# Threshold attention into an RWKV feed-forward: probabilities of 15 of 32 jobs turned on VectorE and by DMA instead of on TensorE

## Chip, core and metric

The kernel runs on one core of one Trainium2 chip. The metric is the device time of one execution in microseconds. Below, PE is TensorE's matmul, PEld its weight load, DVE VectorE, ACT ScalarE, POOL GpSimd and SP the queue of SyncE, which issues every DMA of this kernel. L667 is line 667 of the kernel before; the changed kernel has its own line numbers, and its lines are named as such.

## What is computed

Attention over 8 batches, 8 heads, 576 tokens and 64 columns a head, in which each score below its row's maximum less tau is dropped, and then an RWKV feed-forward over the 512 columns of all heads:

```python
scores = q @ k.T / sqrt(64)
thresh = max(scores, axis=-1) - tau
attn = softmax(where(scores >= thresh, scores, -1e9))
x = (attn @ v), heads side by side            # 8 x 576 x 512
x_prev = x shifted by one token
xk = mu_k * x + (1 - mu_k) * x_prev
xr = mu_r * x + (1 - mu_r) * x_prev
k = maximum(xk @ w_k, 0)                      # 512 -> 1024
out = sigmoid(xr @ w_r) * (k * k @ w_v)
```

All inputs are float32. Products whose rounding matters are made from a high and a low part (fp32r) in three matmuls, or, for attn @ v, in float32 matmuls, each of which the hardware runs as two instructions.

## The kernel before

**Jobs and units.** A job is one pair of heads of one batch; batches 0 and 1 are cut into two jobs a pair, which makes 40 jobs, and 32 pairs in all (the title counts pairs). A job's units are P units, 128 queries of both heads (a score tile of 128 x 576 for each head), and, once a pair, a T unit, the last 64 queries of both heads stacked to 128 rows. Two P units (256 queries) make a group; the T unit goes with one of the two groups.

**A unit's way.** operands() loads q and k of the pair (tile raw), scales, splits into hi and lo (L466, L476) and stacks them by eight DMAs a job into st1 and st2 (L495). scores() multiplies them into the PSUM tile s (L559; for the T unit L534, six matmuls of 288 columns with bd as weights). softmax() takes the row maximum on DVE (L593), the threshold and the exponential on ACT (L601, L609), drops and sums on DVE (L617), inverts the sum (L628, L629) and scales the probabilities p on POOL (L643). turn_pair() then turns p, since attn @ v needs the keys on the partitions: per P unit nine PE transpositions of 128 x 128 (L667), four a head for keys 64 to 575 (the main part) and one for the first 64 keys of both heads (the tail), into PSUM; two copies of 128 x 512, one on ACT (L685) and one on DVE (L687), bring the main part into the tile pm, and one ACT copy the tail into pl. turn_last() does it for the T unit. attend() multiplies pm and pl with v (L747): per group 10 float32 matmuls, 20 instructions, of 256 columns, or 320 where the T unit's 64 queries are in the same tile; DVE copies the result into xT (L687).

**Feed-forward.** ffn_chunk() works on 256 tokens of a batch: POOL differences (L840), DVE mixes into the tile mk (L849), ACT and POOL split into xk and xr (L862, L870), then PE with w_k (L892, 256 columns), w_r (L934) and w_v (L956, 512 columns), and one DMA for 128 rows of output (L972). There are 18 chunks.

**Order.** No engine's order is written by hand. Each step is added with an assumed duration and a key; Plan.order() is a list scheduler that repeatedly takes the step that can start first by these assumptions, ties and near ties (SOFT) by key, and places buffers. The instructions are then issued in that order, and each engine runs its own in order. PE steps of the attention have keys lowered by 1000, so they go ahead of feed-forward steps that could start at the same time. Steps with until (L1012, the fillers) are transpositions of the identity, placed on PE only where the plan sees a gap in the first 100 us.

Of the kernel before, what the change touches and what calls it, by code (L numbers as in the profile page):

```python
# [17 lines left out]
W_MAX = 2.0 ** (0x8F - 127) * (1 + 0x6FFFFF / 2.0**23)  # L18

# [29 lines left out]
class Plan:  # L49
# [4 lines left out]
    SOFT = {"DVE": 0.3, "ACT": 0.3}  # L54
    IDLE = 0.5
# [58 lines left out]
    def order(self, loose=()):  # L114
# [48 lines left out]
        while sum_ < total:  # L163
# [60 lines left out]
def tile_threshold_attention_then_rwkv_ffn(  # L224
# [33 lines left out]
    NE = NTB + 1  # L258
    assert ST == D and NPAIR == NCT and B % NTB == 0
# [10 lines left out]
    W0, W1, W2, W3, AVK = 3.0, 3.5, 50.0, 2.0, 4.5  # L270
    PREP, PB, VB, COLD, EARLY = 8, 2, 2, -1, 30
    EV = ("ACT", 0.49), ("DVE", 0.6)
    KMAX, KEXP, KMASK = 0.0, 0.0, 0.5
# [156 lines left out]
    def operands(job, key):  # L430
        b, hp, nq = job["b"], job["hp"], job["nq"]
        W = nq + 2 * ST + SM
        raw = job["raw"] = sbuf("raw", [P, WM], F32, 2)
# [49 lines left out]
        job["st"] = [(sbuf("st1", [P, WM], FR, 3), sbuf("st2", [P, S], FR, 3)) for _ in range(2)]  # L483
        for h in range(2):
# [4 lines left out]
            for dst, rows, src, n, r in (  # L489
                (t1, up, hi, W, (hi, None)),  # L490
                (t2, dn, hi, nq, (hi, None)),
                (t1, dn, lo, W, (lo, None)),
                (t2, up, lo, nq, (lo, 0)),
            ):
                fn = (lambda dst=dst, rows=rows, src=src, n=n, sl=sl: SY.dma_start(  # L495
                    dst.get()[rows, 0:n].bitcast(F32), src.get()[sl, 0:n].bitcast(F32)
                ))
                add("DMA", DQ, fn, reads=[r], writes=[(dst, rows.start)], key=key - PREP, kb=n // 4)
# [4 lines left out]
    def scores(unit, ss, key):  # L503
        job, c = unit["job"], unit["c"]
        raw, nq = job["raw"], job["nq"]
# [3 lines left out]
        def keys(y, z):  # L509
            k0 = nq + (ST if unit["kind"] == "P" and y == 0 else 0)  # L510
            return slice(k0 + z * HS, k0 + (z + 1) * HS)

        if unit["kind"] == "T" and not job["plain"]:

            hi, lo = job["hi"], job["lo"]
            for v_, src in enumerate((raw, lo)):
                for h in range(2):
# [4 lines left out]
                        lambda v_=v_, src=src, sl=sl: A.activation(  # L522
                            bd.get()[sl, v_, sl], src.get()[sl, nq - ST : nq].bitcast(F32), AF.Copy
# [6 lines left out]
            for j, (v_, r) in enumerate(prods):  # L530

                def mm(j=j, v_=v_, r=r):
                    for z in range(2):
                        PE.matmul(ss[1].get()[:, z, 0:HS], bd.get()[:, v_], r.get()[:, keys(1, z)], start=(j == 0), stop=(j == 2))  # L534

                add("PE", 0.264, mm, reads=[bd, r], writes=[ss[1]], key=key - 1000, lat=0.44)
            return
        if unit["kind"] == "T" or job["plain"]:

            last = unit["kind"] == "T"  # L540

            def both():
                for z in range(2):
                    for h in range(2):
                        hr = slice(h * D, (h + 1) * D)
                        o = ss[1].get()[hr, z, 0:HS] if last else ss[h].get()[:, z, 0:HS]
                        q = slice(nq - ST, nq) if last else slice(c * P, (c + 1) * P)
                        PE.matmul(o, raw.get()[hr, q], raw.get()[hr, keys(h, z)], start=True, stop=True)
# [20 lines left out]
    def softmax(unit):  # L569
# [4 lines left out]
        p = unit["p"] = sbuf("p", [P, 2, S], F32, PB)  # L574
        ss = {y: psum("s", [P, 2, 512], 2) for y in ys}
        scores(unit, ss, float(n))
        for y in ys:
# [3 lines left out]
            def sv(s=s):  # L581
                return s.get()[:, :, 0:HS]

            def pv(y=y):
                return p.get()[:, y].rearrange("p (a b) -> p a b", a=2)

            def col(j, y=y):
# [5 lines left out]
                lambda sv=sv, col=col: V.tensor_reduce(col(0), sv(), axis=AX.XY, op=ALU.max, negate=True),  # L593
# [17 lines left out]
                writes=[(p, y)],  # L611
# [9 lines left out]
                writes=[(p, y), (sm, (2, y))],  # L621
# [17 lines left out]
        for y in ys:  # L639
# [4 lines left out]
                    p.get()[:, y], p.get()[:, y], sm.get()[:, 3, y : y + 1], 0.0, op0=ALU.mult, op1=ALU.add  # L644
                ),
                reads=[(sm, (3, y))],
                writes=[(p, y)],
                key=n - 1.0,
# [4 lines left out]
    def group(job, g):  # L653
        if g not in job["groups"]:
            job["groups"][g] = (
                sbuf("pm", [P, 2, 4, CH + ST], F32, 2),
                sbuf("pl", [P, CH + ST], F32, 2),
# [3 lines left out]
    def transposes(p, y, at, key, to):  # L661
# [3 lines left out]
        def mm():  # L665
            for c, o in enumerate(at):
                PE.transpose(  # L667
                    pt.get()[:, c, :], p.get().rearrange("p y s -> p (y s)")[:, o : o + P], ident.get()
                )

        occ = 0.109 * len(at) * (2.3 if key < COLD else 1)
# [4 lines left out]
            reads=[*((p, z) for z in y), ident],  # L676
# [12 lines left out]

    def turn_pair(unit):  # L690
        n, job, p, c = (unit[j] for j in ("n", "job", "p", "c"))
        pm, pl = group(job, c // 2)
        cs = slice(c % 2 * P, (c % 2 + 1) * P)
        for y in range(2):
            pt = transposes(p, (y,), [y * (S + ST) + j * P for j in range(4)], n + y - 1.0, [(pm, (y, c % 2))])
            evict(
                *EV[y if n > EARLY else 0],
                pt,
                lambda y=y: pm.get()[:, y, :, cs],
                lambda pt=pt: pt.get(),  # L700
                [(pm, (y, c % 2))],
                n + y - 2.0,
            )
        pt = transposes(p, (0, 1), [SM], n + 0.1, [(pl, c % 2)])
        evict("ACT", 0.2, pt, lambda: pl.get()[:, cs], lambda: pt.get()[:, 0], [(pl, c % 2)], n - 1.0)

    def turn_last(unit):
        n, job, p = unit["n"], unit["job"], unit["p"]
        pm, pl = group(job, job["tg"])
        cs = slice(CH, CH + ST)  # L710
# [386 lines left out]
```

## Time and profile before

| | |
|---|---|
| median of 3 runs | 1066.53 us (1066.46 to 1067.39) |
| the profiled execution | 1066.21 us, its span 1064.4 us, mean granted clock 0.995 |
| busy, share of span | PE 97%, PEld 81%, DVE 70%, ACT 69%, POOL 55% |
| idle time on PE | 33.9 us (1064.4 less 1030.5) |
| PE transpositions of p (L667) | 1312 |
| DMA | 118.48 MB, SP's queue 42.9% of 16 engines' span |

Busy time counts an instruction from its start to a modelled end. Matmuls overlap, so the mean of one is longer than what it takes of PE in a row; for that the chain of waits is read, which merges instructions that follow each other without a gap.

### The profile page before, as it was taken

To read this page: it belongs to the slowest core of one execution; us is meant where nothing else is said; L and a number is where in the kernel's file an instruction comes from. 1 tells how busy PE (TensorE), PEld (TensorE's weight loads), DVE (VectorE), ACT (ScalarE), POOL (GpSimd) and SP (SyncE) were. 2 spreads that over 40 slices of the span, in tenths; PEclk is the share of its full clock that TensorE was granted. 3 is DMA by queue.
4 is the path that set the end of the run, shared out by engine and by line. 5 is a ranking of instruction groups with operands and counts; after the bars stand their busy time and mean duration, and the time that the engine had idled before them with its cause. 6 is when DMAs were issued, how large, how long until landed. Compare 5 with 4: busy or idle time off the path is not lost.

```text
span 1064.4 us, 19978 instructions
## 1 busy us (share of the span) xinstructions
PE 1030.5 (97%) x7021; PEld 859.1 (81%) x7021; DVE 744.0 (70%) x1816; ACT 731.8 (69%) x1557; POOL 582.2 (55%) x610
## 2 busy tenths in 40 slices
PE   8999989999999899999999999999999999999998
PEld 6677677787877788878879788787889788888887
DVE  6998777777877878779778888757878497222220
ACT  5889766788777687876777768757786567444442
POOL 4789656555554565555565546464556354344441
PEclk9999999999999999999999999999999999999999
DMA  6895574655444444445545346433643050000000
GB/s 219 238 322 140 135 187 123 167 131 148 126 106 126 106 109 115 119 101 130 126 104 124 98 113 140 100 85 81 163 107 89 13 124 15 20 20 22 20 20 20
DMA packets 44354, 118.48 MB, mean 111 GB/s; under 512 B 7392, under 2 KB 10976, under 8 KB 44256
## 3 DMA queue, kind: packets, MB, share of 16 engines
q1 hardware_dynamic: 44256, 117.21, 42.9%
q8 instruction: 57, 0.93, 0.4%
q14 instruction: 41, 0.34, 0.1%
HBM read 46.14 MB, written 9.44 MB: 52 GB/s over the span
## 4 chain that ended last, share of the span: by engine, by line
PE 80%; DVE 7%; ACT 6%; DMA 3%; issue 2%; POOL 1%; SPq 0%; POOLq 0%; ACTq 0%; DVEq 0%
PE w L892 18%; PE w L956 14%; PE w L747 13%; PE s L559 12%; PE w L667 11%; PE w L934 8%; PE s L534 2%; DVE p L617 2%; ACT p L609 2%; DVE mk L849 2%; DVE sm L593 2%; DMA st<-lo 2%; PE w L1012 1%; ACT pm L685 1%; ACT L609 1%
## 5 line engine op out<-in xcount | busy, mean ns | idle before, releaser
L643 POOL TENSOR_SCALAR p<-p,sm 128x576 f32<-128x576 f32 x288 | 218.8, 771 | 204.5 <-DVE sm L629 130.5
L617 DVE SCALAR_TENSOR_TENSOR p<-s,sm,p 128x576 f32<-128x576 f32 x288 | 233.0, 814 | 64.3 <-ACT p L609 61.9
L892 PE MATMUL w<-xk,wk 128*128 128x256 f32 x1728 | 238.8, 286 | 1.7 <-ACT r L900 1.1
L593 DVE TENSOR_REDUCE sm<-s 128x1 f32<-128x576 f32 x288 | 210.3, 751 | 36.9 <-PE s L559 27.3
L956 PE MATMUL w<-wv,k 128*128 128x512 f32 x864 | 219.8, 396 | 1.7 <-ACT pm L685 1.7
L892 PEld LDWEIGHTS w<-xk,wk 128*128 128x128 f32 x1728 | 219.0, 190 | 2.9 <-ACT r L900 1.3
L609 ACT ACTIVATE p<-s,sm 128x576 f32<-128x576 f32 x288 | 210.6, 732 | 0.5
L667 PE MATMUL w<-ident,p 128*128 128x128 f32 x1312 | 193.2, 276 | 7.5 <-POOL p L643 3.5
L667 PEld LDWEIGHTS w<-ident,p 128*128 128x128 f32 x1312 | 151.6, 141 | 43.0 <-POOL p L643 16.9
L956 PEld LDWEIGHTS w<-wv,k 128*128 128x128 f32 x864 | 155.9, 188 | 29.7 <-ACT pm L685 2.3
L685 ACT ACTIVATE pm<-w 128x512 f32<-128x512 f32 x174 | 102.9, 593 | 76.6 <-PE w L667 75.2
L870 POOL TENSOR_TENSOR xk<-mk,xk 128x512 fp32r<-128x512 f32 x72 | 92.7, 1288 | 111.2 <-ACT xk L862 104.8
L747 PE MATMUL w<-pm,v 128*64 128x256 f32 (+1 forms) x1024 | 142.2, 416 | 1.7 <-DVE pm L687 1.1
L849 DVE SCALAR_TENSOR_TENSOR mk<-m,mu_sb,xT 128x256 f32<-128x256 f32 x128 | 87.5, 723 | 80.0 <-POOL xk L870 78.8
L915 POOL TENSOR_TENSOR k<-r,k 128x512 fp32r<-128x512 f32 x72 | 93.2, 1294 | 89.2 <-ACT k L905 82.2
L601 ACT ACTIVATE sm<-sm,small 128x1 f32<-128x1 f32 x288 | 83.5, 290 | 74.6 <-DVE sm L593 73.3
L559 PE MATMUL s<-st 128*128 128x288 f32 x496 | 115.2, 314 | 13.5 <-issue 5.1
L476 POOL TENSOR_TENSOR lo<-raw,hi 128x576 fp32r<-128x576 f32 (+2 forms) x76 | 105.6, 1408 | 33.2 <-ACT hi L466 25.3
L747 PEld LDWEIGHTS w<-pm,v 128*64 128x64 f32 x1024 | 68.5, 138 | 57.5 <-issue 8.8
L934 PE MATMUL w<-wr,xk 128*128 128x512 f32 x432 | 110.1, 396 | 0.2 <-ACT pm L685 0.2
L559 PE MATMUL s<-st,st 128*128 128x288 f32 x496 | 109.0, 301 | 0.0
L559 PEld LDWEIGHTS s<-st 128*128 128x128 f32 x496 | 79.0, 190 | 31.3 <-issue 14.8
(66 smaller groups left out, 1142.3 us busy)
## 6 DMA issues: line engine op xcount, KB each, us to landing
raw<-in_qk SPq DMA_DIRECT2D x24, 608.0 KB, 4.8
st<-hi SPq DMA_DIRECT2D x48, 304.0 KB, 3.2
st<-lo SPq DMA_DIRECT2D x48, 304.0 KB, 4.2
v<-in_v SPq DMA_DIRECT2D x40, 320.0 KB, 4.0
out<-sg SPq DMA_DIRECT2D x32, 256.0 KB, 2.1
st<-hi SPq DMA_DIRECT2D x48, 144.0 KB, 3.4
st<-lo SPq DMA_DIRECT2D x48, 144.0 KB, 3.7
wk<-in_w_k SPq DMA_DIRECT2D x8, 512.0 KB, 6.4
```

The source lines that it names most:

```text
L559: PE.matmul(ss[y].get()[:, z, 0:HS], l.get()[:, c * P : (c + 1) * P], r.get()[:, keys(y, z)], start=(j == 0), stop=(j == 1),)
L593: lambda sv=sv, col=col: V.tensor_reduce(col(0), sv(), axis=AX.XY, op=ALU.max, negate=True),
L609: lambda sv=sv, pv=pv, col=col: A.activation(pv(), sv(), AF.Exp, bias=col(0)),
L617: lambda sv=sv, pv=pv, col=col: V.scalar_tensor_tensor(pv(), sv(), col(1), pv(), op0=ALU.is_ge, op1=ALU.mult, accum_out=col(2)),
L643: lambda y=y: G.tensor_scalar(p.get()[:, y], p.get()[:, y], sm.get()[:, 3, y : y + 1], 0.0, op0=ALU.mult, op1=ALU.add),
L667: PE.transpose(pt.get()[:, c, :], p.get().rearrange("p y s -> p (y s)")[:, o : o + P], ident.get())
L685: fn = lambda: A.activation(out_(), in_(), AF.Copy)
L747: PE.matmul(o.get()[hs, 0:n], vt.get()[:, c, hs], pt[:, 0:n], start=(c == 0), stop=(c == 4))
L849: V.scalar_tensor_tensor(d.get()[:, y, o : o + n], diff.get()[:, y, o : o + n], mu_sb.get()[:, j, hc + y : hc + y + 1], prv[:, hc + y], op ...
L892: PE.matmul(h.get()[:, f], l, r, start=(ct == 0 and i == 0), stop=(ct == NCT - 1 and i == 2))
L934: PE.matmul(z.get(), l, r, start=(ct == 0 and i == 0), stop=(ct == NCT - 1 and i == 2))
L956: PE.matmul(vps.get(), l, r, start=(ft == 0 and i == 0), stop=(ft == NFT - 1 and i == 2))
```

## The change

**Moved jobs.** For batches 3 to 7 and the first three of the four pairs (15 pairs) the main part is no longer turned by PE. DVE turns both heads' 512 main columns of a unit in place, each 32 x 32 block by itself (one STREAM_TRANSPOSE of 128 x 2 x 512 a unit, 60 in all), and when both units of a group are done, 16 DMAs a group from SP carry the rows of blocks to their partitions in pm, each 32 partitions of four pieces of 512 bytes, 64 KB (480 in all). The host orders queries and the rows of v to match. The tail is still turned by PE. For the other 17 pairs PE still turns everything, into the new layout.

**Layout.** p holds a whole group now (two buffers, each for two units, where it was one unit each), pm is 128 x 8 x 2 x 128, and the T unit has its own tiles pml and pll; attend() therefore has 10 matmuls of 256 columns and, with a T unit, 10 more of 64 columns, where it had 10 of 320. The T unit's scores are three matmuls of 512 and three of 64 columns, where they were six of 288. Where a job has a T unit, its 64 queries come first, and st1 and st2 lose those 64 columns.

**Buffers and numbers.** raw has one buffer, not two (job 1 borrows k2); the tile mk is gone: the second mix is written over the difference m, the first into a buffer of r; r keeps two. Constants of the planner differ (SOFT, IDLE, W1 2.5 instead of 3.5, KMAX 1 instead of 0, the attend key's 2.5 instead of 1.5); the planner is told 0.5 us for the issue of one of the 16 DMAs. The T unit leads in the second half jobs.

Counts by the two orders: PE transpositions of p 1312 to 832; PE fillers of three 63 to 52; copies of 128 x 512 into pm on DVE 114 to 54 and on ACT 142 to 82; T-unit copies 32 on ACT as before; DMAs on SP gain the 480; activation table loads 26 to 30.

The core of the diff:

```diff
+def moved(b, hp):
+    return b >= 3 and hp < 3
...
-    SOFT = {"DVE": 0.3, "ACT": 0.3}
-    IDLE = 0.5
+    SOFT = {"DVE": 0.15, "ACT": 0.4, "POOL": 0}
+    IDLE = 0.7
...
-                s.end = max(t + 3.5, pipe + 2.5)
+                s.end = max(t + s.occ + 3.0, pipe + 2.5)
...
+    KTURN, KMOVE, RB, DMOVE = 1, 4, 2, 0.5
+    KMAX, KEXP, KMASK = 1, 0, 0.5
...
-                    for z in range(2):
-                        PE.matmul(ss[1].get()[:, z, 0:HS], bd.get()[:, v_], r.get()[:, keys(1, z)], start=(j == 0), stop=(j == 2))
+                    k = r.get()[:, nq : nq + S]
+                    main = k[:, ST:]
+                    if job["moved"]:
+                        main = main.rearrange("p (r c a) -> p c r a", c=4, a=Q)
+                    for o, x in ((ss[1].get()[:, 0], main), (ss[1].get()[:, 1, 0:ST], k[:, 0:ST])):
+                        PE.matmul(o, bd.get()[:, v_], x, start=(j == 0), stop=(j == 2))
...
+        if job["moved"]:
+
+            def turn():
+                x = strided(p.get()[:, t * PW :], 2, SM)
+                V.transpose(x, x)
+
+            add("DVE", 1.13, turn, writes=[(p, (t, y, "m")) for y in range(2)], key=n - KTURN)
...
+        if job["moved"] and t == 1:
+            for r in range(NQ):
+
+                def move(r=r):
+                    for i in range(NQ):
+                        SY.dma_start(
+                            pm.get()[r * Q : (r + 1) * Q, 2 * i : 2 * i + 2].rearrange("p t h n -> p (t h) n"),
+                            strided(p.get()[i * Q : (i + 1) * Q, r * P :], 4, P),
+                        )
+
+                add("DMA", NQ * DMOVE, move, reads=[(p, (z, y, "m")) for z in range(2) for y in range(2)], writes=[(pm, (r, "moved"))], key=n - KMOVE, kb=256)
...
-            for c in cs:
-                for h in range(2):
-                    hs = slice(h * D, (h + 1) * D)
-                    pt = pl.get() if c == 4 else pm.get()[:, h, c]
-                    PE.matmul(o.get()[hs, 0:n], vt.get()[:, c, hs], pt[:, 0:n], start=(c == 0), stop=(c == 4))
+            for a, e, pm, pl in parts:
+                for c in cs:
+                    for h in range(2):
+                        hs = slice(h * D, (h + 1) * D)
+                        pt = pl.get() if c == 4 else pm.get()[:, :, h, c * Q : (c + 1) * Q]
+                        PE.matmul(o.get()[hs, a:e], vt.get()[:, c, hs], pt, start=(c == 0), stop=(c == 4))
...
-            for j in range(2):
-                d = sbuf("mk", [P, 2, CH], F32, 1)
+            for j in (1, 0):
+                d = sbuf("r", [P, 2, CH], F32, RB) if j else diff
```

**PE before, a job of batch 3.** From the attend of one group (pm_0_4966 with the T unit's columns) over the next T unit's scores (s_0_5198) to the nine transpositions of a P unit's probabilities (p_1_5174); wv are weights of the feed-forward.

```order
L747 MATMUL w_1_5176<-pm_0_4966,v_1_4650 64x320 x8
L747 MATMUL w_1_5176<-pl_0_4973,v_1_4650 64x320 x2
L667 MATMUL w_0_5196<-ident_66,p_0_5078 128x128
L534 MATMUL s_0_5198<-hi_0_4869,bd_81 128x288 x2
L534 MATMUL s_0_5198<-lo_0_4888,bd_81 128x288 x2
L534 MATMUL s_0_5198<-hi_0_4869,bd_81 128x288 x2
L559 MATMUL s_1_5211<-st1_1_4890 128x288 x2
L559 MATMUL s_1_5211<-st1_1_4890,st2_1_4901 128x288 x2
L667 MATMUL w_2_5221<-ident_66,p_1_5174 128x128 x4
L956 MATMUL w_3_5112<-wv50_0_1665,k2_0_4731 128x512 x3
L667 MATMUL w_0_5238<-ident_66,p_1_5174 128x128 x4
L667 MATMUL w_1_5250<-ident_66,p_1_5174 128x128
```

The main part's transpositions are the two rows with x4, between other work.

**PE now, the first moved job (batch 3).** The next T unit's scores (s_0_4685), the scores ahead of them, and behind them all that PE still turns of a P unit of this job (p_1_4593), the tail.

```order
L574 MATMUL s_1_4674<-st1_1_4309,st2_1_4318 128x288 x2
L547 MATMUL s_0_4685<-hi_0_4415,bd_81 128x512
L547 MATMUL s_0_4685<-hi_0_4415,bd_81 128x64
L547 MATMUL s_0_4685<-lo_0_4435,bd_81 128x512
L547 MATMUL s_0_4685<-lo_0_4435,bd_81 128x64
L547 MATMUL s_0_4685<-hi_0_4415,bd_81 128x512
L547 MATMUL s_0_4685<-hi_0_4415,bd_81 128x64
L692 MATMUL w_1_4700<-ident_66,p_1_4593 128x128
```

The T unit's scores alternate 512 and 64 columns where three rows of x2 with 288 stood, and the P unit's two rows with x4 are gone.

**PE now, the same job's two groups.** From the last tail transposition of the second group (p_1_4593) to the attend of the first (pm_0_4694 with pl, then the T unit's pml and pll).

```order
L692 MATMUL w_1_4789<-ident_66,p_1_4593 128x128
L1024 MATMUL w_2_4783<-wv10_0_1335,k2_0_4368 128x512 x3
L1024 MATMUL w_2_4783<-wv20_0_1433,k2_0_4368 128x512 x3
L1024 MATMUL w_2_4783<-wv30_0_1515,k2_0_4368 128x512 x3
L1024 MATMUL w_2_4783<-wv40_0_1784,k2_0_4368 128x512 x3
L1024 MATMUL w_2_4783<-wv50_0_1851,k2_0_4368 128x512 x3
L816 MATMUL w_3_4829<-pm_0_4694,v_0_4198 64x256 x8
L816 MATMUL w_3_4829<-pl_0_4600,v_0_4198 64x256 x2
L816 MATMUL w_3_4829<-pml_0_4505,v_0_4198 64x64 x8
L816 MATMUL w_3_4829<-pll_0_4513,v_0_4198 64x64 x2
L574 MATMUL s_0_4862<-st1_0_4644 128x288 x2
L574 MATMUL s_0_4862<-st1_0_4644,st2_0_4649 128x288 x2
```

The second group's attend (pm_1_4799) stands behind these rows, two further rows of scores with x2, two triples with wv (L1024), five transpositions, six triples of L960 and four rows of scores with x2; it reads what the 16 DMAs of p_1_4593 bring.

**SP before, around the same place.** Stacking DMAs (st), and the next pair's loads.

```order
L495 DMA st1_0_4795<-hi_0_4524 64x1216
L495 DMA st2_0_4806<-hi_0_4524 64x576
L495 DMA st1_0_4795<-lo_0_4530 64x1216
L495 DMA st2_0_4806<-lo_0_4530 64x576
L495 DMA st1_1_4890<-hi_0_4869 64x1216
L495 DMA st2_1_4901<-hi_0_4869 64x576
L495 DMA st2_1_4901<-lo_0_4888 64x576
L495 DMA st1_1_4890<-lo_0_4888 64x1216
L437 DMA raw_1_4940<-in_qk 128x1216
L454 DMA v_0_4949<-in_v 128x640
```

Eight stacking DMAs, raw and v are a job's whole share of the queue beside the outputs.

**SP now, the first moved job.** The same queue with the 16 DMAs of each of its two groups (L761).

```order
L502 DMA st1_0_4644<-lo_0_4435 64x1152
L502 DMA st2_0_4649<-lo_0_4435 64x512
L761 DMA pm_0_4694<-p_0_4439 32x4x128 x16
L502 DMA st1_1_4787<-hi_0_4705 64x1152
L502 DMA st2_1_4795<-hi_0_4705 64x512
L761 DMA pm_1_4799<-p_1_4593 32x4x128 x4
L1040 DMA out_0<-sg_0_4672 128x512
L761 DMA pm_1_4799<-p_1_4593 32x4x128 x12
L502 DMA st1_1_4787<-lo_0_4720 64x1152
L502 DMA st2_1_4795<-lo_0_4720 64x512
L444 DMA raw_0_4919<-in_qk 128x1216
```

The second group's DMAs are cut into 4 and 12 by an output, which waits for a feed-forward product; stacking DMAs of the next job stand behind both groups.

More of the change, by code (lines that the diff above doesn't have):

```diff
@@ L675, in transposes @@
             mm,
-            reads=[*((p, z) for z in y), ident],
+            reads=[*r, ident],
             writes=[pt, *to],
@@ L688, in evict, with strided, main @@
         add(eng, occ, fn, reads=[pt], writes=w, key=key)
+    def strided(x, k, n):
+        return bass.AP(x.tensor, x.offset, [list(x.ap[0]), [PW // 2, k], [1, n]])
+    def main(p, o, c):
+        return lambda: p.get()[:, o + c * P : o + (c + 1) * P]
     def turn_pair(unit):
[L691 to L702, printed above, removed]
-            )
@@ L704, in turn_pair @@
-        pt = transposes(p, (0, 1), [SM], n + 0.1, [(pl, c % 2)])
-        evict("ACT", 0.2, pt, lambda: pl.get()[:, cs], lambda: pt.get()[:, 0], [(pl, c % 2)], n - 1.0)
+        n, job, p, t, g = (unit[j] for j in ("n", "job", "p", "t", "g"))
+        pm, pl = group(job, g)
+        if job["moved"]:
+            def turn():
+                x = strided(p.get()[:, t * PW :], 2, SM)
+                V.transpose(x, x)
+            add(
+                "DVE",
+                1.13,
+                turn,
+                writes=[(p, (t, y, "m")) for y in range(2)],
+                key=n - KTURN,
+            )
+        else:
+            for y in range(2):
+                pt = transposes([main(p, t * PW + y * (PW // 2), c) for c in range(4)], [(p, (t, y, "m"))], n + y - 1.0, [(pm, (y, t))])
+                evict(
+                    *EV[y if n > EARLY else 0],
+                    pt,
+                    lambda y=y: pm.get()[:, :, y].rearrange("p (i t) (c q) -> p t c i q", t=2, q=Q)[:, t],
+                    lambda pt=pt: pt.get().rearrange("p c (i q) -> p c i q", q=Q),
+                    [(pm, (y, t))],
+                    n + y - 2.0,
+                )
@@ new lines, in turn_pair @@
+        pt = transposes([main(p, t * PW + SM, 0)], [(p, (t, y, "t")) for y in range(2)], n + 0.1, [(pl, t)])
+        evict(
+            "ACT",
+            0.2,
+            pt,
+            lambda: pl.get().rearrange("p (i t q) -> p t i q", t=2, q=Q)[:, t],
+            lambda: pt.get()[:, 0].rearrange("p (i q) -> p i q", q=Q),
+            [(pl, t)],
+            n - 1.0,
+        )
+        if job["moved"] and t == 1:
[5 more added lines that the diff above has]
+                            strided(p.get()[i * Q : (i + 1) * Q, r * P :], 4, P),
+                        )
+                add(
+                    "DMA",
+                    NQ * DMOVE,
+                    move,
+                    reads=[(p, (z, y, "m")) for z in range(2) for y in range(2)],
+                    writes=[(pm, (r, "moved"))],
+                    key=n - KMOVE,
+                    kb=256,
+                )
@@ L707, in turn_last @@
     def turn_last(unit):
-        n, job, p = unit["n"], unit["job"], unit["p"]
-        pm, pl = group(job, job["tg"])
-        cs = slice(CH, CH + ST)
-        pt = transposes(p, (1,), [S + ST + c * P for c in range(4)], n - 1.0, [(pm, (0, 2)), (pm, (1, 2))])
+        n, job, p, t = (unit[j] for j in ("n", "job", "p", "t"))
+        pm, pl = job["last"] = sbuf("pml", [P, 2, 2, P], F32), sbuf("pll", [P, ST], F32)
+        pt = transposes([main(p, t * PW + S, c) for c in range(4)], [(p, (t, 1, "m"))], n - 1.0, [pm])
@@ L735, in attend @@
         n = CH + (ST if job["tail"] and job["tg"] == g else 0)
-        pm, pl = job["groups"][g]
+        parts = [(0, CH, *job["groups"][g])] + ([(CH, n, *job["last"])] if n > CH else [])
         vt = job["v"]
@@ L757, in attend @@
                 lambda cs=cs: mm(cs),
-                reads=[vt, pm, pl],
+                reads=[vt, *(x for part in parts for x in part[2:])],
                 writes=[o, *(free if j == 0 else [])],
```

134 lines of the change are left out of this document (81 added, 53 removed).

## The prediction

> **What bounds the kernel now.** I read the page's shares first, then its chain of waits.
>
> ```profile
> span 1064.4 us, 19978 instructions
> ...
> PE 1030.5 (97%) x7021; PEld 859.1 (81%) x7021; DVE 744.0 (70%) x1816; ACT 731.8 (69%) x1557; POOL 582.2 (55%) x610
> ...
> PE 80%; DVE 7%; ACT 6%; DMA 3%; issue 2%; POOL 1%; SPq 0%; POOLq 0%; ACTq 0%; DVEq 0%
> ```
>
> PE is busy nearly throughout and carries four fifths of the chain; no other engine passes 70%. Next the stretches, by windows (for each: length, then busy time and count of PE, PEld, DVE, ACT, POOL, granted clock, DMA share, GB/s).
>
> ```profile
> 0.00:150.00 150.00, 135.04 (x912) 106.78 (x913) 122.92 (x291) 117.07 (x253) 108.55 (x123) 0.98 0.72 207
> 150.00:350.00 200.00, 194.29 (x1348) 158.63 (x1346) 152.91 (x372) 148.60 (x327) 110.26 (x114) 1.00 0.54 136
> 350.00:900.00 550.00, 541.38 (x3820) 452.60 (x3819) 433.37 (x1074) 400.19 (x873) 298.97 (x316) 1.00 0.43 104
> 900.00:1064.00 164.00, 159.81 (x950) 141.14 (x948) 34.82 (x81) 65.89 (x106) 64.41 (x59) 1.00 0.06 20
> ```
>
> Batches 3 to 7, where the moved jobs are, lie in the third stretch: PE idles 8.6 of 550 us. In the last 164 us only feed-forward is left (DVE 34.8 us). So attention can run somewhat late without costing anything, as long as feed-forward of an earlier batch is there for PE: the end is set by the sum of PE's work plus the moments at which its fixed order makes it wait. I therefore count PE.
>
> What an instruction takes of PE in a row is read from the chain in order of time (start, length, group, number):
>
> ```profile
> 399.95 2.08 PE w L956 x9
> ...
> 403.16 2.84 PE w L747 x20
> ...
> 406.27 0.81 PE s L534 x6
> ...
> 424.99 0.55 PE w L667 x5
> ...
> 435.83 2.31 PE w L747 x20
> ...
> 438.84 1.06 PE s L559 x8
> 439.90 2.84 PE w L892 x24
> ...
> 469.67 0.98 PE w L667 x9
> ```
>
> That is 231 ns for 512 columns (2.08/9), 118 for 256 (2.84/24), 132 for 288 scores, 109 for a transposition (0.98/9; 0.55/5 gives 110), and for a whole attend 2.31 us at 256 columns and 2.84 at 320.
>
> **Part by part. 1, transpositions gone.** 1312 less 832 are 480 on PE, at 109 ns: 52.3 us. The upper bound is the group's busy time:
>
> ```profile
> L667 PE MATMUL w<-ident,p 128*128 128x128 f32 x1312 | 193.2, 276 | 7.5 <-POOL p L643 3.5 <-DVE xT L410 1.4 <-POOL lo L476 0.8
> ```
>
> 193.2/1312 is 147 ns, or 70.7 us; but that share holds modelled ends, under which the next matmul already runs. I take **-52.3**.
>
> **2, the T unit's own attend.** 32 attends of 320 columns (2.84 us) become one of 256 (2.31) and 20 instructions of 64 columns. No row has these. The line through the two attends gives 0.72 us for them (8.3 ns a column, 0.19 fixed), net +0.19; at the 109 ns of a transposition, the shortest matmul in the trace, 2.18, net +1.65. Their weights are 64 columns and the transposition's 128, so I take half of the latter, 1.09: net +0.56, times 32 **+17.9** (ends 6 and 53).
>
> **3, the T unit's scores.** Six of 288 columns are 0.81 us. Three of 512 are 0.69; three of 64 are 0.10 by the line through 118 and 231 ns (5 ns plus 0.44 a column), or 0.35 if one cannot be shorter than 118 ns, since every matmul loads 128 columns of weights first. That is -0.02 to +0.23. Weight loads of this width last as long beside 256 columns as beside 512:
>
> ```profile
> L892 PEld LDWEIGHTS w<-xk,wk 128*128 128x128 f32 x1728 | 219.0, 190 | 2.9 <-ACT r L900 1.3 <-ACT pm L685 1.1
> L956 PEld LDWEIGHTS w<-wv,k 128*128 128x128 f32 x864 | 155.9, 188 | 29.7 <-ACT pm L685 2.3
> ```
>
> So I take the upper end, 0.23 times 32: **+7.4** (ends -0.6 and 7.4).
>
> **4, PE's waits that go.** PE and its weight load wait for POOL's scaling ahead of transpositions:
>
> ```profile
> PEld w L667 <- POOL p L643: 16.9, 35, 1.6
> PE w L667 <- POOL p L643: 3.5, 7, 1.4
> ```
>
> 480 of 1312 go; of 16.9 that is **-6.2** (of 3.5 it would be -1.3). What is late next is the moved data, term 5.
>
> **5, the wait that comes.** attend() of a moved group stands in PE's fixed order behind work that has to cover DVE's turn, 16 issues on SP and the last landing. The cover, from the group's last tail transposition to its attend, in the order shown for pm_1_4799: seven triples of 512 columns 4.9, the first group's attend 2.31 and its T piece 1.09, four rows and four rows of scores 2.1, five transpositions 0.55, six triples of 256 columns 2.1: 13.1 us. Counted so, the 30 groups have 8.3 to 14.6, mean 12.05. The need: the nearest rows for the turn are DVE's copies of 512 and 256 columns,
>
> ```profile
> L687 DVE COPY pm<-w 128x512 f32<-128x512 f32 x114 | 78.2, 686 | 33.5 <-PE w L667 32.4
> L687 DVE COPY xT<-w 128x256 f32<-128x256 f32 x64 | 26.8, 419 | 27.5 <-PE w L747 27.1
> ```
>
> 1.04 ns a column, so 1.22 us for 1024; for issues and landings the stacking DMAs (min, median, max in ns on SP; KB each and median us to landing):
>
> ```profile
> L495 SPq DMA_DIRECT2D st<-hi x152: 461/568/1526, 20.4 to 874.9; - x152
> ...
> st<-lo SPq DMA_DIRECT2D x48, 304.0 KB, 4.2
> ...
> st<-hi SPq DMA_DIRECT2D x12, 64.0 KB, 2.9
> ```
>
> 16 at 461 ns are 7.4, at the median 9.1; landing 2.9 to 4.2. The need is 11.5 to 14.5. I take 11.5, since the 16 are alike and stand behind one another: nine covers fall short, by 13.2 us in all: **+13.2** (ends 0, if the turn is done before the tail's transposition, and 73.6).
>
> **6, the start.** PE fillers, which stand in gaps that the plan sees in the first 100 us, fall from 63 threes to 52. 33 times 109 ns is **-3.6**; the threshold IDLE rose too, so the ends are 0 and, with the second raw buffer gone, +5 as a guess at one lost load.
>
> **At nothing.** DVE loses 60 copies of 686 ns and gains 60 turns of 1.22 us: 433 us of the 550 become 465, hidden under PE's 541. ACT loses 60 copies, POOL nothing. DMA gains 480 x 64 KB, 31.5 MB on 117.2; in proportion to bytes the share 0.43 of that stretch becomes about 0.65. SP's queue gains 221 us (480 x 461 ns) in 550; what is queued behind a group's DMAs are the next job's stacking DMAs, for which scores wait, and an output may stand between, which waits for its product. Mixing without mk shortens a chain beside PE.
>
> The turn also waits on DVE for POOL's scaling, and behind it stand the next units' maxima and masked products, for which PE's scores wait. Cover: other DVE work is placed between; if that fails it is rival B's case.
>
> **The sum.** The profiled execution took 1066.2 us (span 1064.4 and 1.8 around it), 0.3 under the median of 1066.5. 1066.2 - 52.3 + 17.9 + 7.4 - 6.2 + 13.2 - 3.6 = **1042.6 us**.
>
> **Rivals.**
>
> *A, the moves land late (slower).* Place: the attends of moved groups. At 568 ns an issue and 3.7 us to landing the need is 14.0, and the 30 covers fall short by 59.1 us, 45.9 more than counted: 1088.5. The gain without term 5 is 36.8, so it decides from a need of 13.2 us. For it: the queue's median, and pieces of 512 bytes, while the smallest stacking pieces are 1 KB. Against it: a DMA of 64 KB lands sooner (2.9) than one of 304 KB (4.2).
> The Trainium skill, "Perfetto Trace Analysis", DMA Optimizations, speaks against this change: transfers under about 2 KB have a significant overhead each. "DMA: Bandwidth & Descriptors", Why small descriptors are slow (HBM only), exempts copies within SBUF, which these are. No run here has shown 512-byte pieces; by the first page it would be case A, by the second the forecast.
>
> *B, DVE becomes tight.* Turns read and write SBUF while POOL does. Two-input mixes from SBUF, by their distribution and their group's mean:
>
> ```profile
> L849 DVE SCALAR_TENSOR_TENSOR mk<-m,mu_sb,xT x128: 466/482/1773, 43.8 to 999.9; 128x256 f32<-128x256 f32 x128
> ...
> L849 DVE SCALAR_TENSOR_TENSOR mk<-m,mu_sb,xT 128x256 f32<-128x256 f32 x128 | 87.5, 723 | 80.0 <-POOL xk L870 78.8 <-POOL m L840 0.8
> ```
>
> Their mean is 1.55 times the least. So the turn would take 1.9 us, the need 12.2 (20 us short, +7), and DVE 506 of 550 us, which leaves little between dependent steps; if a quarter of the 0.7 us times 60 reaches PE, another 10: 1060.
> The Trainium skill, "SBUF — State Buffer", SBUF: two separate sides, calls the port that DVE and GpSimd share an exclusive lock, held for an instruction, when DVE reads two SBUF inputs or runs a 2-port mode. The mixes' maximum of 1773 ns agrees; a turn has one input, and no run here shows its mode.
>
> *C, the small pieces are cheap and the moves hidden.* Terms 2, 3 and 5 at their lower ends: 6, -0.6 and 0: 1066.2 - 52.3 + 6 - 0.6 - 6.2 - 3.6 = 1009.5. For it: PE waited for few things before.
>
> **How the numbers follow.** Forecast (1025 to 1055) 0.55, C 0.18, B 0.12, A 0.11, no change to speak of 0.04. The forecast is the likeliest case's sum. The range goes down to just under C, 1008, and up over B to 1066; only A and mere accidents are left out. 0.2%, some 2.1 us, is about what a measurement of this kernel can tell from no change. Faster: forecast, C and B, 0.85; same 0.04; slower 0.11.
>
> **What would show it.** Busy PE falls by about 25 us or more, L692 (transpositions now) has 832; the T unit's attend takes near 1.1 us in the chain, its scores near 1.05. Term 5 shows in waits of PE at L816 for DMA: near 13 us if right, over 50 in case A. A turn (L726) near 1.2 us clears B. The prediction is wrong if PE's work falls as counted but the idle time on PE grows by more than 25 us, or if the small pieces cost nothing.

## The result, and the profile after

The changed kernel takes 1082.65 us (median of 4 runs, 1081.04 to 1085.8) beside 1066.96 for the kernel before on the same chip: ratio 1.0144, 95% interval 1.0113 to 1.0175. It is slower by 15.7 us; 1042.6 was forecast, in a range up to 1066. The page of its profiled execution (1085.8 us, span 1084.0) answers to the first lines shown of before:

```profile
span 1084.0 us, 20907 instructions
...
PE 1008.1 (93%) x7148; PEld 846.3 (78%) x7148; DVE 763.3 (70%) x1816; ACT 718.6 (66%) x1501; POOL 583.2 (54%) x610
...
PE 48%; SPq 18%; DVE 11%; DMA 8%; issue 6%; ACT 5%; POOL 3%; POOLq 0%; DVEq 0%; ACTq 0%
SPq L761 15%; PE w L960 11%; PE w L816 9%; PE w L1024 9%; PE s L574 7%; PE w L692 6%; PE w L1002 4%; DVE p L637 3%; SPq L502 3%; DMA st<-lo 2%; DVE sm L613 2%; DMA raw<-in_qk 2%; DMA pm<-p 2%; POOL p L663 2%; PE s L547 1%
```

PE's busy time fell by 22.4 us, as it should. But its idle time rose from 33.9 us (1064.4 less 1030.5) to 75.9, and the chain names what stands there: SP's queue had 0% of it and has 18%, 15% in L761 alone, the line that issues the 16 DMAs of a group. The windows show where (length, then busy time and count of PE, PEld, DVE, ACT, POOL, granted clock, DMA share, GB/s):

```profile
350.00:900.00 550.00, 503.23 (x3531) 422.64 (x3531) 400.95 (x930) 353.25 (x735) 284.76 (x291) 0.98 0.60 142
900.00:1064.00 164.00, 158.29 (x1065) 137.14 (x1065) 71.57 (x178) 85.78 (x159) 73.50 (x73) 0.99 0.23 56
```

In the stretch of the moved jobs PE idles 46.8 us, where it idled 8.6. DVE does not fill up (400.95 us, less than before in this stretch, since attention runs behind: it still has 71.57 us to do after 900, where it had 34.82). The DMA engines are at 0.60, so what is full is neither of them. The view of L761, and SP's timeline around two groups (start, length, and how many instructions):

```profile
L761 SPq DMA_DIRECT2D pm<-p x480: 585/599/1966, 350.1 to 958.1; - x160
...
  ACT p L629: 30.9, 17
  PE w L816: 26.8, 15
  POOL lo L483: 19.0, 5
  ACT L629: 9.9, 4
...
DMA to landing us min/median/max: 2.0/2.1/5.8
```

```profile
564.03 11.29 SPq L761 DMA_DIRECT2D pm<-p  x16
575.43 1.19 SPq L502 DMA_DIRECT2D st<-lo  x2
576.66 0.76 SPq L444 DMA_DIRECT2D raw<-in_qk  x1
...
609.91 10.35 SPq L761 DMA_DIRECT2D pm<-p  x16
```

One issue takes 599 ns at the median and never under 585; the prediction had taken 461. A group's 16 occupy the queue for 10.35 to 11.29 us, and the next stacking DMAs and raw load begin directly behind them (at 575.43 and 576.66). The landing, 2.1 us, is shorter than the 2.9 that was priced. One attend in the chain in order of time:

```profile
498.47 0.60 SPq L761
...
501.05 0.60 SPq L761
502.33 2.10 DMA pm<-p
504.44 1.02 issue
505.46 4.08 PE w L816 x20
```

Issues of 0.60 us each, the last one's landing, and then an attend that takes 4.08 us in place of 2.31. Why it is longer is in the windows over this attend and over one, at 459.09, that did not wait (2.31 us for the same 20 instructions); the clock is the sixth column after the length:

```profile
505.40:509.60 4.20, 4.14 (x21) 2.77 (x22) 1.16 (x6) 2.36 (x4) 2.31 (x3) 0.59 0.03 6
459.00:461.40 2.40, 2.40 (x22) 1.42 (x22) 1.29 (x6) 2.32 (x7) 1.88 (x2) 1.00 0.90 186
```

In PE's timeline a gap stands ahead of the long one:

```profile
505.46 3.62 PE L816 MATMUL w<-pm,v 128*64 128x256 f32 x16 [3.33 <-issue]
```

PE stood idle for 3.33 us, and behind that the granted clock is 0.59 (0.50 from 506.4 to 508.4 us, 1.00 again from 509.4). This wait is paid twice: once idle, and 1.77 us more in slow matmuls. It is not alone: between 340 and 960 us six attends stand behind gaps of 2.63 to 3.33 us, and the clock over them is 0.50 to 0.64. The waits by engine:

```profile
ACT raw L452 <- DMA raw<-in_qk: 31.8, 12, 7.8
ACT p L629 <- DMA pm<-p: 30.9, 17, 4.3
...
PE w L816 <- DMA pm<-p: 19.4, 12, 3.2
```

The wait at the attend (19.4 us here; 26.8 in the view of L761 above) is only the first of three. ACT waits 31.8 us for raw loads that stand behind the moves on SP, and 30.9 us with an exponential, because the p tile that it writes is still being read by them. In the kernel before, the wait for raw loads was small:

```profile
ACT raw L445 <- DMA raw<-in_qk: 2.4, 2, 2.0
```

### The profile page after: what moved, and what is told of

Read it like the earlier page. It is cut to its first block, busy times and chain, and to the rows that moved or that the text cites. A ratio compares the mean times of both kernels' runs of the same rounds, so it can differ in the third digit from the quotient of the medians.

```text
span 1084.0 us, 20907 instructions
## 1 busy us (share of the span) xinstructions
PE 1008.1 (93%) x7148; PEld 846.3 (78%) x7148; DVE 763.3 (70%) x1816; ACT 718.6 (66%) x1501; POOL 583.2 (54%) x610
## 4 chain that ended last, share of the span: by engine, by line
PE 48%; SPq 18%; DVE 11%; DMA 8%; issue 6%; ACT 5%; POOL 3%; POOLq 0%; DVEq 0%; ACTq 0%
SPq L761 15%; PE w L960 11%; PE w L816 9%; PE w L1024 9%; PE s L574 7%; PE w L692 6%; PE w L1002 4%; DVE p L637 3%; SPq L502 3%; DMA st<-lo 2%; DVE sm L613 2%; DMA raw<-in_qk 2%; DMA pm<-p 2%; POOL p L663 2%; PE s L547 1%
## 5 line engine op out<-in xcount | busy, mean ns | idle before, releaser
L960 PE MATMUL w<-xk,wk 128*128 128x256 f32 x1728 | 231.6, 284 | 0.7 <-ACT pm L708 0.6
L629 ACT ACTIVATE p<-s,sm 128x576 f32<-128x576 f32 x288 | 209.3, 730 | 31.9 <-DMA pm<-p 30.9
L1024 PE MATMUL w<-wv,k 128*128 128x512 f32 x864 | 222.9, 402 | 0.4 <-ACT pl L708 0.4
L960 PEld LDWEIGHTS w<-xk,wk 128*128 128x128 f32 x1728 | 215.9, 188 | 2.6 <-ACT pm L708 1.1
L1024 PEld LDWEIGHTS w<-wv,k 128*128 128x128 f32 x864 | 158.2, 191 | 32.7 <-ACT pl L708 0.8
L816 PE MATMUL w<-pm,v 128*64 128x256 f32 x1024 | 134.7, 405 | 33.1 <-DMA pm<-p 19.4
L692 PE MATMUL w<-ident,p 128*128 128x128 f32 x832 | 136.2, 281 | 12.0 <-POOL p L663 5.4
L816 PEld LDWEIGHTS w<-pm,v 128*64 128x64 f32 x1024 | 76.0, 143 | 77.2 <-issue 41.2
L692 PEld LDWEIGHTS w<-ident,p 128*128 128x128 f32 x832 | 97.5, 142 | 37.7 <-POOL p L663 15.9
L1002 PEld LDWEIGHTS w<-wr,xk 128*128 128x128 f32 x432 | 78.6, 190 | 14.6 <-issue 0.4
L726 DVE STREAM_TRANSPOSE p<-p 128x1024 f32<-128x1024 f32 x60 | 74.2, 1238 | 11.2 <-POOL p L663 11.1
L574 PEld LDWEIGHTS s<-st,st 128*128 128x128 f32 x496 | 80.2, 192 | 2.1 <-issue 1.3
```

The lines of the kernel that those rows point to most:

```text
L574: PE.matmul(ss[y].get()[:, z, 0:HS], l.get()[:, c * P : (c + 1) * P], r.get()[:, keys(y, z)], start=(j == 0), stop=(j == 1),)
L629: lambda sv=sv, pv=pv, col=col: A.activation(pv(), sv(), AF.Exp, bias=col(0)),
L692: PE.transpose(pt.get()[:, c, :], x(), ident.get())
L816: PE.matmul(o.get()[hs, a:e], vt.get()[:, c, hs], pt, start=(c == 0), stop=(c == 4))
L960: PE.matmul(h.get()[:, f], l, r, start=(ct == 0 and i == 0), stop=(ct == NCT - 1 and i == 2))
L1002: PE.matmul(z.get(), l, r, start=(ct == 0 and i == 0), stop=(ct == NCT - 1 and i == 2))
```

## The experiments

**Theory I**: what limits is the time that SP's queue takes to issue, about 0.6 us for each of these DMAs whatever it carries; 16 a group are too many, for the attend and for the loads behind them. The rivals, each as its expectation numbers it, blame something else: the new order, layout or single raw buffer; the bytes or the small pieces; the crossing of partitions. The kernel before took 1066.7 to 1067.4 us beside each group of runs.

**no_moves**: after's layout, constants and buffers, but no job moved.

```diff
-    return b >= 3 and hp < 3
+    return False
```

> The changed kernel with no job moved: its layout, buffers, separate T tiles and planner constants stay, but TensorE turns every job's probabilities and SP issues none of the 480 small DMAs. Theory I (the issue of 16 DMAs a group on SP is what costs): the 480 transpositions return, about 52 us of TensorE's work, but its waits fall back to those of the kernel before (idle about 35 us instead of 76); with the T pieces at about 10 us the time is 1066 to 1082 us. Theory II (the single buffer for the raw loads and the rest of the layout make TensorE wait): the idle time stays near 76 us and the work comes on top, 1120 us or more.

1074.74 us (1073.44 to 1076.37), ratio 1.0071, 1.0048 to 1.0093. Its page:

```profile
span 1074.4 us, 21089 instructions
...
PE 1038.1 (97%) x7628; PEld 885.4 (82%) x7628; DVE 726.8 (68%) x1816; ACT 741.6 (69%) x1557; POOL 578.3 (54%) x610
```

PE idles 36.3 us, 2.4 more than before. So the layout, the single raw buffer and the constants cost some 8 us by the medians (10.0 between the profiled spans, 7.6 of it busy PE), and hardly any of the 42.0 us that PE idles more in after. ACT's wait for raw loads is 2.4 us here, as before, though there is one buffer.

**issue_known**: after, with the planner told 0.65 us an issue in place of 0.5.

```diff
-    KTURN, KMOVE, RB, DMOVE = 1, 4, 2, 0.5
+    KTURN, KMOVE, RB, DMOVE = 1, 4, 2, 0.65
```

> The changed kernel, with the planner told 0.65 us for the issue of one of the 16 DMAs instead of 0.5, so that it orders all engines by what the trace shows. Theory I (SP's queue itself is too slow for the moved stage): the order cannot make the queue faster, a group still takes 10.4 us of it; small gain, 1065 to 1082 us. Theory III (only the order is wrong, since the plan believed 0.5 us): TensorE's waits fall back to about 35 us idle, near 1043 us.

1072.35 us (1066.34 to 1075.79, 10 runs), ratio 1.0047, 1.0024 to 1.0069, in theory I's range. An order made with the true price gains some 10 us on after, but SP's queue keeps 13% of the chain and L761 its 585/599 ns. Part of the loss is the order's, not the larger part.

**quarter_issues**: after's order, bytes and partitions written, but each four of the 16 DMAs are one of 256 KB within the same 32 partitions, in pieces of 2 KB. The exchange of blocks between partitions is left out.

```diff
-                    for i in range(NQ):
-                        SY.dma_start(
-                            pm.get()[r * Q : (r + 1) * Q, 2 * i : 2 * i + 2].rearrange("p t h n -> p (t h) n"),
-                            strided(p.get()[i * Q : (i + 1) * Q, r * P :], 4, P),
-                        )
+                    SY.dma_start(
+                        pm.get()[r * Q : (r + 1) * Q].rearrange("p a h n -> p (a h n)").rearrange("p (x n) -> p x n", n=SM),
+                        strided(p.get()[r * Q : (r + 1) * Q, 0:], 4, SM),
+                    )
```

> The changed kernel in the same order on every engine, but each four of the 16 DMAs of a group become one of the same 256 KB that copies within the same 32 partitions, so 120 issues instead of 480. It leaves out the exchange of blocks between partitions. Theory I: a group takes about 3 us of SP instead of 10.4, no attend waits for it, and loads behind it are on time: 1040 to 1055 us. Theory II (the raw buffer and layout): stays at 1075 us or more, since the same loads still have one buffer. A theory of bandwidth (the bytes moved delay other DMAs): the bytes are the same, so also 1075 or more.

1017.34 us (1015.73 to 1020.47), ratio 0.9536, 0.9508 to 0.9563: 65 us under after, and below the 1040 to 1055 that theory I had expected. This alone doesn't settle it, as three things changed at once: the number of issues, the size of the pieces, and the crossing of partitions. Two more runs part them.

**same_partitions**: all 16 issues and pieces of 512 bytes, but no crossing.

```diff
-                            strided(p.get()[i * Q : (i + 1) * Q, r * P :], 4, P),
+                            strided(p.get()[r * Q : (r + 1) * Q, i * P :], 4, P),
```

> All 16 DMAs of 64 KB in pieces of 512 bytes, in after's order, but each copies within the 32 partitions that it reads; the exchange of blocks across partitions is left out. Theory I (SP's queue takes 0.6 us for each of the 16 issues): nothing changes, 1075 to 1090, L761 x480 near 585/599. Theory II (carrying data from partitions to other partitions is what is slow): as in the run with a quarter of the issues, 1015 to 1030, and the landing falls below 2.1 us.

1086.24 us (1083.97 to 1089.79), ratio 1.0185, 1.0161 to 1.0209. No gain at all: crossing partitions is not what costs. The three waits are there as in after:

```profile
ACT raw L452 <- DMA raw<-in_qk: 31.8, 14, 7.7
ACT p L629 <- DMA pm<-p: 30.4, 21, 3.8
...
PE w L816 <- DMA pm<-p: 16.1, 14, 3.2
```

**quarter_512**: four issues as in quarter_issues, pieces of 512 bytes as in after, no crossing. Each DMA spans all 128 partitions, where those of after and of quarter_issues write 32.

```diff
-                    for i in range(NQ):
-                        SY.dma_start(
-                            pm.get()[r * Q : (r + 1) * Q, 2 * i : 2 * i + 2].rearrange("p t h n -> p (t h) n"),
-                            strided(p.get()[i * Q : (i + 1) * Q, r * P :], 4, P),
-                        )
+                    SY.dma_start(
+                        pm.get()[:, 2 * r : 2 * r + 2].rearrange("p t h n -> p (t h) n"),
+                        strided(p.get()[:, r * P :], 4, P),
+                    )
```

> Four DMAs of 256 KB a group over 128 partitions, in the pieces of 512 bytes that after has (the earlier run with a quarter of the issues had pieces of 2 KB); the exchange across partitions is left out. Theory I: only the number of issues counts, 1012 to 1030. Theory III (pieces of 512 bytes are slow): between 1045 and 1085, with landings well over 4.7 us and PE waiting at its attend for DMA by more than 10 us.

1018.75 us (1017.82 to 1020.47), ratio 0.9554, 0.9539 to 0.9570: the same as quarter_issues. Its page, its stretch of moved jobs and its move line:

```profile
PE 984.7 (97%) x7148; PEld 829.8 (82%) x7148; DVE 764.2 (75%) x1816; ACT 717.7 (71%) x1501; POOL 583.3 (57%) x610
...
PE 76%; DVE 11%; ACT 5%; issue 2%; POOL 2%; DMA 2%; SPq 0%; POOLq 0%; ACTq 0%; DVEq 0%
```

```profile
350.00:900.00 550.00, 543.95 (x3978) 459.41 (x3978) 451.72 (x1046) 395.60 (x823) 317.37 (x325) 1.00 0.60 155
```

```profile
L760 SPq DMA_DIRECT2D pm<-p x120: 594/652/1474, 349.4 to 885.4; - x120
...
DMA to landing us min/median/max: 2.6/3.5/7.0
```

The DMA share is 0.60 as in after, the bytes and pieces are the same, and yet PE idles 6.1 of 550 us in place of 46.8. An issue of 256 KB takes 652 ns where one of 64 KB takes 599: it is priced by the DMA, hardly by what it carries. Between same_partitions and quarter_512 the bytes and pieces are alike and no block crosses; 16 issues or four a group is the difference, and it is 67.5 us. A DMA also spans 128 partitions in place of 32 here, but quarter_issues, with 32, takes the same time. No engine waits for pm<-p any more, and ACT's wait for raw loads, with the same single buffer, is back to what it was before:

```profile
ACT raw L452 <- DMA raw<-in_qk: 2.1, 3, 1.2
```

Theory I is shown for the loss as a whole; how much each of the three waits passes on to PE was not parted.

Could the change be had with fewer issues, or with time between them? Nothing is left out in these.

**by_hbm**: the blocks go through a scratch tile in HBM, four DMAs of 256 KB out and four in, with 0.65 in the planner.

```diff
+                    lambda r=r: SY.dma_start(
+                        box.get()[r].rearrange("p (x n) -> p x n", n=P), strided(p.get()[:, r * P :], 4, P)
+                    ),
...
+                    lambda r=r: SY.dma_start(
+                        pm.get()[r * Q : (r + 1) * Q].rearrange("p (i t) h n -> p i (t h n)", t=2),
+                        box.get()[r].rearrange("(i a) n -> a i n", i=NQ),
+                    ),
```

> The changed kernel with the exchange done through HBM: per group four DMAs of 256 KB write p to a scratch and four read it back to the right partitions, 8 issues instead of 16 of about 0.6 us, but two landings in a row; planner told 0.65 us. Theory I: SP spends about 5 us a group instead of 10.4, and the way from turn to landing is about 1.2 + 2.6 + 2.5 + 0.6 + 4 = 11 us instead of 13.7: 1045 to 1065 us. Theory II, or a theory of bandwidth (bytes of the exchange double): 1080 us or more.

1061.04 us (1057.63 to 1066.17, 10 runs), ratio 0.9947, 0.9927 to 0.9967. Half the issues, and faster than before; but DMA now has 13% of the chain, and its share in the stretch is 0.84:

```profile
350.00:900.00 550.00, 513.84 (x3662) 434.92 (x3660) 435.23 (x1002) 368.82 (x780) 298.74 (x307) 0.98 0.84 208
```

**alternate_ten** and **first_two**: after's moves for ten jobs, planner at 0.65. In alternate_ten an unmoved job stands behind each moved one; in first_two the two stand together.

```diff
-    return b >= 3 and hp < 3
+    return b >= 3 and hp in (0, 2)
```

> Only 10 pairs moved, the first and the third of each batch from 3 on, so that a job turned by TensorE stands between two moved ones; planner told 0.65 us an issue. From no move (1075 us) to a quarter of the issues (1017 us) a moved job is worth 3.8 us where nothing waits. Theory I (SP's queue is filled by 32 issues of 0.65 us within a job's time): the queue drains during the job between, few waits are left, 1075 - 38 = 1037, so 1035 to 1055 us. A theory of lateness alone (each move is late against its attend by the same amount, whatever stands between): 10 of 15 parts of the loss remain, about 1037 + 37 = 1074 us.

```diff
-    return b >= 3 and hp < 3
+    return b >= 3 and hp < 2
```

> The same 10 pairs' worth, but the first two of each batch, so two moved jobs stand next to each other, then two turned by TensorE; planner told 0.65 us. Theory I (the queue fills up over neighbouring moved jobs): slower than with the moved jobs apart, 1045 to 1065 us. A theory in which only the number of moves counts: the same time as with them apart, within 4 us.

alternate_ten 1053.4 us (1049.39 to 1055.58), ratio 0.9869, 0.9831 to 0.9907; first_two 1057.68 (1052.94 to 1059.41), ratio 0.9905, 0.9873 to 0.9937; both in theory I's ranges. Fewer moves are faster than 15; SP's share of the chain is 6% in both. Whether the spacing adds to that is open, since the intervals overlap.

**half_on_act**: 15 jobs, half of each group's DMAs issued on ACT's queue, planner at 0.65.

```diff
+                act = r % 2
...
+                        (A if act else SY).dma_start(
...
+                    "ACT" if act else "DMA",
```

> All 15 pairs moved, with half of the 16 DMAs of a group issued from ScalarE's queue instead of SP's, the planner told 0.65 us on either. SP spends 5.2 us a group instead of 10.4; ScalarE, 719 us busy, gets 240 issues of about 0.6 us, 150 us more, in its fixed order. Theory I (what costs is the issue time on the one queue): the moved data land about 5 us sooner, TensorE's idle time shrinks; 1035 to 1060 us, if ScalarE does not become tight. A theory that the DMA engines or the small pieces themselves are slow: no change, 1070 to 1083 us.

1181.41 us (1180.61 to 1183.42), ratio 1.1075, 1.1048 to 1.1101: the worst of all. The move line on ACT's queue, and the waits over all engines:

```profile
L763 ACTq DMA_DIRECT2D pm<-p x240: 592/616/1731, 352.3 to 1004.1; - x120
```

```profile
DVE p L637 <- ACT p L629: 153.7, 98, 8.8
...
ACT pl L708 <- DMA pm<-p: 123.5, 21, 7.3
...
PE s L574 <- DVE p L637: 79.3, 32, 10.7
```

An issue costs ACT the same 0.6 us, but ACT works in order: 240 of them, 148 us by the median, stand between its exponentials, DVE's masks wait 153.7 us for those and PE's scores 79.3 for the masks. The 123.5 us that ACT idles ahead of copies of the tail are these issues once more, since issuing does not count as busy: at 352.34 eight of them take 5.42 us, and the copy behind them shows 5.35 us of idle time. Neither theory's number for this run came: here the second queue had work behind it that others wait for.

**alternate_fourteen**: jobs 0 and 2 of batches 1 to 7.

```diff
-    return b >= 3 and hp < 3
+    return b >= 1 and hp in (0, 2)
```

> Jobs 0 and 2 of batches 1 to 7 are moved, with 16 DMAs a group and 0.65 in the planner for each. Theory I: the spacing counts and not the number of jobs, so the four more jobs bring their 128 transpositions at 109 ns, up to 14 us less than the ten (1053): 1040 to 1053. Rival: in the first 350 us the queue and the DMA engines still carry the feed-forward's weights, and the moves wait among them: 1054 to 1075.

1100.47 us (1098.05 to 1101.4), ratio 1.0312, 1.0294 to 1.0329: slower than either expectation allowed. Its first stretches with moved jobs:

```profile
150.00:350.00 200.00, 181.86 (x1262) 150.80 (x1263) 133.84 (x317) 129.12 (x276) 99.74 (x102) 0.95 0.59 145
350.00:900.00 550.00, 512.89 (x3731) 432.22 (x3731) 412.65 (x989) 371.91 (x790) 290.87 (x304) 0.97 0.55 132
```

PE idles 18.1 us of the 200, where before idles 5.7 and has no moves there, and 37.1 of the 550, where alternate_ten idles 17.6 (550 less 532.38). That fits attention that falls behind early and never catches up; which transfer begins it was not tried.

**alternate_ten_hbm**: by_hbm with the jobs of alternate_ten.

> Two unmoved jobs no longer stand side by side: jobs 0 and 2 of batches 3 to 7 are moved, and their blocks go through a scratch tile in HBM, four DMAs out and four in. Theory I: fewer issues than 16 and time between the groups, 1035 to 1052. Rival: DMA engines are as full as in the run of 15 jobs by HBM (share 0.84), and the loads that wait for them cost as much: 1053 to 1062, no gain over the ten jobs with 16 DMAs.

1058.59 us (1057.68 to 1062.07), ratio 0.9929, 0.9908 to 0.9949: the rival's number, no gain on alternate_ten. The DMA share fell to 0.70 and PE still waits 8.7 us for the blocks from HBM, so a full set of DMA engines isn't all that slows this route.

**staged_hbm**: by_hbm, with turns that write the blocks in the order in which they are sent. A scratch tile takes the place of the second pm buffer.

```diff
-                x = strided(p.get()[:, t * PW :], 2, SM)
-                V.transpose(x, x)
+                for r in range(NQ):
+                    V.transpose(tu.get()[:, r, 2 * t : 2 * t + 2], strided(p.get()[:, t * PW + r * P :], 2, P))
```

> 15 moved jobs; four turns of 256 columns per pair of units write the turned blocks to a tile of their own in the order in which they are sent (it takes the place of the second pm buffer in moved jobs), so that two DMAs of 512 KB in pieces of 4 KB carry a group out to HBM and four of 256 KB in pieces of 2 KB back: six issues a group in place of sixteen, or of eight with pieces of 512 bytes. Theory I (issues): 1030 to 1050, below the run of 15 jobs by HBM with eight issues (1061), SP's issues near 0% of the chain. Rival (every byte goes twice, and the landings of DMAs this large, 5 us or more each way, end last): 1055 to 1075, with waits of PE at its attend for the DMA from HBM of 15 us or more.

1051.8 us (1051.16 to 1057.93), ratio 0.9878, 0.9834 to 0.9922: between the two expectations. PE's wait at the attend for these DMAs is gone (first row), the turns in four cost hardly more than in one (second; 240 of 410 ns beside 60 of 1238):

```profile
PE w L831 <- DMA pm<-box: 3.8, 6, 1.0
```

```profile
L731 DVE STREAM_TRANSPOSE pm<-p 128x256 f32<-128x256 f32 x240 | 84.1, 410 | 3.7 <-POOL p L664 2.0
```

Some 33 us remain to quarter_512; the page puts 7% of the chain on DMA and 8% on ACT. What they consist of stays open. With alternate_ten this is the fastest whole version: both beat the kernel before, and they can't be told apart.

## Why the prediction was wrong, point by point

Without term 5 the sum is 1029.4 us; quarter_512, in which nothing waits for the moves, takes 1018.75. So the other terms were 10.7 us too high together, and the wait, put at 13.2 us, was 63.9 (1082.65 less 1018.75), 50.7 too low. The two errors have opposite signs and leave the 40 us by which the forecast missed.

- **Terms 1 and 4, transpositions and their waits: right.** quarter_issues is no_moves without 480 transpositions and with turns and moves that cost PE nothing: 57.4 us less (1074.74 to 1017.34), where -52.3 and -6.2 make 58.5. In the profiled executions PE's busy time falls by 51.3 us and its idle time by 6.1.
- **Term 2, the T unit's own attend: too high.** Forecast +17.9, ends 6 and 53. The 40 instructions take 2.89 us in a row, 0.05 more than the 20 of 320 columns, 1.6 us in 32 attends: below the lower end. A piece of 64 columns takes 29 ns (0.58/20); the transposition, with columns and weights twice as many, was a poor neighbour. The Trainium skill, "TensorE: Matmul & The Clock Gate", Back-to-back issue gap, gives columns/2.4 + 2.5 ns at full clock, by estimate 29 for 64, and adds that this is too little for small matmuls that load weights. Here the 29 hold, weights loaded and all, and by them the term would have been near. But for the transposition's 128 columns the same formula gives an estimate of 56 ns, where the trace has 109, so it could not be trusted ahead of the run.
- **Term 3, the T unit's scores: the mechanism right, the size near.** 0.95 us in a row beside 0.81, 0.14 times 32: 4.5 for 7.4. In after:

```profile
189.42 2.89 PE w L816 x40
197.74 0.95 PE s L547 x6
```

- **Term 5, the wait that comes: here it failed.** The step was "I take 11.5, since the 16 are alike and stand behind one another", and that 461 ns is an issue's price. It is the minimum of another DMA; 16 that stand behind one another take 10.35 us, not 7.4. The need is 1.24 + 10.35 + 2.1 = 13.7 us, past the 13.2 from which rival A decides. The term is 64 us (after less quarter_512; 68.0 in the profiled spans, of which 44.6 is PE's idle time, 75.9 less 31.3, and 23.4 is busy time of the same 7148 matmuls, at a mean granted clock of 0.979 beside 0.995). That is within its ends of 0 and 73.6 and near A's 59.1, in part by luck, since A put all of it at the attend. A's time of 1088.5 is 6 over the result because the rest of its sum was 10.7 too high and its wait 4.8 too low.
- **"At nothing": wrong for SP's queue.** The sum listed 221 us more on SP and the loads queued behind, and gave no price for them. At 599 ns it is 288 us. PE's wait at the attend for the moves is 19.4 us; raw loads that come late and p tiles that stay held cost ACT 31.8 and 30.9 us, and through the softmax they reach PE, how much by each was not parted. Slow matmuls behind long gaps come on top, though the trace before had one such gap: 3.03 us of idle PE ahead of 354.53, and a clock of 0.62 in the 2 us behind it. A count of covers at one consumer sees none of these.
- **Rival B: cleared.** A turn takes 1.24 us, as term 5 had it, not 1.9:

```profile
L726 DVE STREAM_TRANSPOSE p<-p x60: 1204/1239/1249, 342.0 to 946.2; 128x1024 f32<-128x1024 f32 x60
```

- **Rival C: the right sum for a kernel without the wait.** 1009.5 beside 1017.34 and 1018.75; but the moves are not hidden at 16 issues. Term 6, the start, wasn't tried by itself; no_moves puts it, terms 2 and 3 and the rest of the layout at 7.7 us together (1074.74 less 1067.05), where the sum had 21.7.
- **What would show it.** Busy PE by -22.4 of 25, and idle PE by +42.0: the text's own mark for wrong, work as counted and idle time up by over 25 us, is what came. A's mark of over 50 us at L816 did not (19.4, or 26.8 by the other view), since the loss spread over three waits.
- **The pages on DMA.** The Trainium skill, "Perfetto Trace Analysis", DMA Optimizations, says that DMAs under 2 KB have a significant overhead each. The prediction applied this to pieces of 512 bytes, though each DMA carries 64 KB, and took it as a sign of case A: the right sign and not the cause, as kernels with 512-byte and with 2 KB pieces take the same time here (1018.75 and 1017.34). The same section says that balancing DMAs across issuing engines may help where descriptor generation is the bottleneck; with ACT at 66% that made 1181.41. "DMA: Bandwidth & Descriptors", Anatomy of one DMA — SWDGE (gpsimd) path, says of DMAs issued from GpSimd that completion, not setup, dominates the fixed cost. For one DMA on SP that holds too (2.1 us beside 0.6); for 16 in a row it does not, since landings overlap and issues add up.

## What to carry to other kernels

Price a group of DMAs on one queue as their number times the issue time of the nearest DMA at its median, never its minimum, and only then add one landing (here even the median, 568 ns, gave 9.1 us where 10.35 came: 0.60 for an issue and 0.04 between two); size and pieces come second. Charge a queue that fills up to everything that stands behind it, loads and held buffers too, not just to the consumer of the new transfers. A second issuing queue helps only if the engine that owns it has nothing behind the issues that others wait for.

## What the runs showed of the hardware that was not expected

- An issue on SP of a copy within SBUF takes 585 to 599 ns for 64 KB and 594 to 652 ns for 256 KB (minimum and median), on ACT's queue 592 to 616.
- A float32 matmul instruction of 64 columns in an attend takes 29 ns in a row, where 256 columns take 115 (2.31/20).
- Behind 3.33 us of idle PE the granted clock was 0.59 over a whole attend (4.08 us in place of 2.31). In after between 340 and 960 us, three gaps of 2.27 to 2.46 us left it at 1.00, and six from 2.63 us on did not; in same_partitions it was 0.62 behind a gap of 2.33 and 1.00 behind one of 3.08, so the length of the gap alone does not decide. The Trainium skill, "TensorE: Matmul & The Clock Gate", What's actually happening, has the clock fall to a half after an idle window of about 3.4 us; the trace agrees in the half (0.50 from 506.4 to 508.4 us), but here shorter gaps were enough.
- Pieces of 512 bytes within SBUF (quarter_512, 1018.75 us) cost no time that these runs can tell from pieces of 2 KB (quarter_issues, 1017.34). The DMAs differ in their partitions too: with 512 bytes and 128 partitions one lands in 3.5 us, with 2 KB and 32 partitions in 4.7.
